# Linear attention: the key-value product folded into the output weight, denominators by column-tiled matmuls, their inverses broadcast by DMA onto the query features

## Chip, cores, metric

One core of one Trainium2 chip. The metric is device time in microseconds (us). "Clock" is the granted TensorE clock that the trace records, 1.00 being full speed. PE is the matrix engine, DVE the vector engine, ACT the scalar engine, POOL GpSimd, SP the engine that issues DMA here, PEld the weight loads of PE. PE writes its results to PSUM, which is used here in banks of 128x512 values. A q behind an engine's name (SPq) marks its sequencer, which waits and issues DMA.

## The reference

Two pre-layernorm blocks follow each other: a linear attention (S = 2048 tokens, D = 1024, 32 heads of 32) and a token-mixing MLP (F = 3584), called the mixer below. Only the end of the attention matters here:

```python
phi = lambda t: jnp.where(t > 0, t + 1, jnp.exp(t)) + 1e-6
pq, pk = phi(q), phi(k)
kv  = jnp.einsum("bhsd,bhse->bhde", pk, v)          # per head 32x32
z   = jnp.einsum("bhsd->bhd", pk)
num = jnp.einsum("bhqd,bhde->bhqe", pq, kv)
den = jnp.einsum("bhqd,bhd->bhq", pq, z)[..., None] + 1e-6
o   = num / den
h   = x + o.transpose(...).reshape(B, S, D) @ wo
# then h2 = h + MLP over tokens of layernorm(h)
```

## The kernel before

Queries are made in 32 units (u, j): 512 tokens (block u of 4) by 128 features (j of 8). Each unit is eight 128x512 matmuls into a PSUM bank, then phi: two ACT operations, then two DVE operations that write `pqT`.

```python
def phi_parts(dst, src, n, pool):
    ...
    def act():
        pin(nc.scalar.activation(e_sb[:], src, ACT.Exp))
        pin(nc.scalar.activation(r_sb[:], src, ACT.Relu))
    def dve():
        pin(nc.vector.tensor_scalar(e_sb[:], e_sb[:], 1.0, PHI_EPS, ALU.min, ALU.add))
        pin(nc.vector.tensor_tensor(dst, e_sb[:], r_sb[:], ALU.add))
def q_unit(u, j):
    qp = acc_tile()                       # one of five PSUM banks
    for kt in range(ND):
        nc.tensor.matmul(qp[:, 0:SW], lhsT=wq_sb[:, kt, j*P:(j+1)*P],
                         rhs=xnT[:, kt, u*SW:(u+1)*SW], start=(kt == 0), stop=(kt == ND-1))
    phi_evac(pqT[:, j, u*SW:(u+1)*SW], qp[:, 0:SW], SW, a2k)   # a2k: four buffers
```

`pin` keeps an operation where the program has it. The others may be reordered on their engine by the compile-time scheduler. Then, for each of 16 tiles of 128 tokens, small matmuls give numerator and denominator side by side; the division and a DMA transpose put o where `pqT` was; the output projection follows.

```python
def attn_num_den(i):
    for j in range(ND):
        nc.tensor.matmul(nd_ps[:, b, sl*NCOL:(sl+1)*NCOL],           # 128 x 132
                         lhsT=pqT[:, j, i*P:(i+1)*P], rhs=ndrhs[:, j, :], start=True, stop=True)
    # ACT: rd = exp(-ln(den)); DVE: o_sb = num * rd (three operations out of PSUM)
    ...
def attn_transpose(i, o_sb):
    nc.sync.dma_start_transpose(out=pqT[:, :, i*P:(i+1)*P], in_=o_sb[:])
...
for (u, j) in q_units[8:]:
    q_unit(u, j)
    if u >= 1 and j % 2 == 1:
        attn((u - 1) * TPC + j // 2)      # attn = attn_transpose(i, attn_num_den(i))
        ...                               # weight loads
for i in range(NS):
    if i % 2 == 0 and i // 2 < TPC:
        attn(NS - TPC + i // 2)
    ...
    out_proj(i)                           # two groups of eight 128x512 matmuls with wo_sb
    ...
```

## Time and profile before

| | before |
|---|---|
| time, median (range) | 573.22 us (573.16 to 573.3, 3 runs) |
| span profiled | 571.5 us |
| PE / DVE / ACT busy | 99% / 68% / 48% |
| from the first query unit after the last kv accumulation to the first matmul of the mixer | 125.92 to 235.50 us |

The last row is the stage that the change touches; I call it "the stage". In it all numbers are taken from PE's timeline, from the start of one group of matmuls to the start of the next.

A stretch of nearly the whole stage, kernel before. The columns are the stretch and its length, busy time and (instructions) of PE, PEld, DVE, ACT and POOL, then granted clock, DMA share, GB/s.

```profile
126.00:236.00 110.00, 110.00 (x605) 53.59 (x603) 86.35 (x210) 74.80 (x179) 0.00 (x0) 1.00 0.61 157
```

PE's timeline before around one group of the small matmuls: start, duration (both us), engine, line, operation, output and inputs, shapes, count.

```profile
136.75 1.89 PE L1019 MATMUL acc_t<-xnT,wq_sb 128*128 128x512 bf16 x8
138.47 0.63 PE L1118 MATMUL nd_ps<-ndrhs,pqT 128*128 128x132 bf16 x8
138.94 1.24 PE L1019 MATMUL acc_t<-xnT,wq_sb 128*128 128x512 bf16 x5
```

PE never pauses in the stage, at full clock. A group of eight small matmuls lasts 0.63 us, but what follows it starts 138.94 - 138.47 = 0.47 us after it: durations overlap, so costs on PE must be read from starts. Sixteen such groups are 16 x 0.47 = 7.5 us.

### The profile page before, as it was taken

Reading aid. Unit: us, or ns where it says so; the run is one execution under the profiler, and the core shown is the slowest. Engines: PE = TensorE matmul, PEld = TensorE weight load, DVE = VectorE, ACT = ScalarE, POOL = GpSimd, SP = SyncE. Lnnn points to the kernel's source line nnn. Section 1 sums busy time; section 2 is a strip of 40 time slices with the busy share of each in tenths; the row PEclk is TensorE's granted clock in tenths of the full one; section 3 lists DMA queues with packets and bytes.
Section 4 is the critical chain, followed back from the end, with each engine's and each line's share of the span. In section 5 each row is a group of like instructions: output and inputs, shape, how many; then the busy total and the mean of one; then the engine's idle time right before and its main releaser. Section 6 shows DMA issues by size and latency. Waiting matters only on the chain.

```text
span 571.5 us, 8308 instructions
## 1 busy us (share of the span) xinstructions
PE 563.7 (99%) x3124; PEld 293.3 (51%) x3124; DVE 390.2 (68%) x759; ACT 272.0 (48%) x585; POOL 1.8 (0%) x8
## 2 busy tenths in 40 slices
PE   7999999999999999999999999999999999999997
PEld 3444444455554444346555565555445655645643
DVE  6898887546767879873735627453979749659625
ACT  4747777666667776445445354453220411311211
POOL 1000000000000000000000000000000000000000
PEclk9999999999999999999999999999999999999999
DMA  9933432029536753104041340413892932912111
GB/s 303 357 76 79 89 74 38 19 96 323 118 72 127 177 178 111 55 2 147 1 148 28 120 148 1 148 48 81 205 255 84 244 96 75 278 56 73 38 47 46
DMA packets 97800, 66.61 MB, mean 117 GB/s; under 512 B 32082, under 2 KB 91744, under 8 KB 97760
## 3 DMA queue, kind: packets, MB, share of 16 engines
q1 hardware_dynamic: 97024, 65.42, 41.7%
q10 hardware_dynamic: 672, 0.66, 0.3%
q8 instruction: 24, 0.39, 0.3%
q14 instruction: 16, 0.13, 0.1%
q0 software_dynamic: 64, 0.01, 0.0%
HBM read 50.34 MB, written 8.39 MB: 103 GB/s over the span
## 4 chain that ended last, share of the span: by engine, by line
PE 95%; DVE 3%; ACT 1%; issue 1%; DMA 1%; ACTq 0%
PE psB L297 10%; PE psC L297 10%; PE acc_t L1019 9%; PE acc_t L1167 9%; PE psC L208 7%; PE psA L297 7%; PE psI L230 7%; PE psB L208 6%; PE psI L208 6%; PE psB L750 4%; PE psC L750 4%; PE psA L750 4%; PE psA L208 3%; PE acc_t L674 2%; PE psE L750 2%; PE psE L297 1%
## 5 line engine op out<-in xcount | busy, mean ns | idle before, releaser
L297 PEld LDWEIGHTS <-sa 128*128 128x128 f16 x436 | 42.6, 98 | 46.8 <-issue 0.7
L1019 PE MATMUL acc_t<-xnT,wq_sb 128*128 128x512 bf16 x256 | 58.0, 379 | 0.0
L1167 PE MATMUL acc_t<-wo_sb,pqT 128*128 128x512 bf16 x256 | 56.1, 379 | 0.0
L208 PEld LDWEIGHTS <-wq 128*128 128x128 bf16 (+1 forms) x357 | 34.5, 98 | 31.3
L297 PEld LDWEIGHTS <-wq 128*128 128x128 bf16 (+1 forms) x324 | 31.6, 98 | 33.1 <-issue 1.0
L208 PE MATMUL psC<-gs,wq 128*128 128x512 f16 (+2 forms) x210 | 45.0, 365 | 0.0
L1167 PEld LDWEIGHTS <-pqT 128*128 128x128 bf16 x256 | 24.8, 98 | 29.0
L1019 PEld LDWEIGHTS <-wq_sb 128*128 128x128 bf16 x256 | 24.5, 98 | 27.4
L166 ACT ACTIVATE e_sb<-acc_t 128x512 bf16<-128x512 f32 x40 | 23.9, 597 | 26.5 <-PE acc_t L1019 24.3
L170 DVE TENSOR_SCALAR e_sb<-e_sb 128x512 bf16<-128x512 bf16 x64 | 18.5, 289 | 25.4 <-ACT e_sb L166 24.8
L208 PEld LDWEIGHTS <-sa 128*128 128x128 f16 x231 | 22.6, 98 | 18.6
L750 PEld LDWEIGHTS <-xs 128*128 128x128 f16 x208 | 20.0, 98 | 23.3 <-DVE xs L736 1.3
L208 DVE TENSOR_TENSOR ot<-ot,hr 128x512 bf16<-128x512 bf16 (+2 forms) x27 | 11.2, 415 | 28.1 <-ACT ot L406 27.7
L333 ACT COPY psC<-psB 128x512 f32<-128x512 f32 x22 | 12.5, 570 | 35.1 <-PE psB L297 21.5
L297 PE MATMUL psB<-hT,sa 128*128 128x512 f16 x112 | 28.4, 379 | 0.0
L441 DVE TENSOR_TENSOR e<-psI,es 128x256 f32<-128x256 f32 x12 | 5.1, 425 | 34.0 <-PE psI L230 34.0
L297 PE MATMUL psC<-hT,wq 128*128 128x512 f16 x112 | 28.3, 379 | 0.0
L750 PE MATMUL psA<-wkv,xnT 128*128 128x512 bf16 x104 | 26.7, 379 | 0.0
L1178 DVE BATCH_NORM_STATS2 hst<-acc_t 128x6 f32<-128x512 f32 x32 | 22.1, 692 | 6.7 <-ACT h_bf L1177 6.5
L297 PE MATMUL psA<-hO,wq 128*128 128x512 f16 x112 | 25.6, 379 | 0.7 <-ACT psB L316 0.7
L297 PE MATMUL psB<-hO,sa 128*128 128x512 f16 x112 | 25.5, 379 | 0.0
L297 PE MATMUL psC<-hT,sa 128*128 128x512 f16 x112 | 25.5, 379 | 0.0
(184 smaller groups left out, 1022.9 us busy)
## 6 DMA issues: line engine op xcount, KB each, us to landing
wq<-in_B_w_dram SPq DMA_DIRECT2D x14, 1024.0 KB, 7.7
wq<-in_B_w_dram SPq DMA_DIRECT2D x8, 1792.0 KB, 9.1
xr<-in_A_x_dram SPq DMA_DIRECT2D x16, 256.0 KB, 3.1
h_dram<-h_bf SPq DMA_DIRECT2D x16, 256.0 KB, 2.2
hr<-h_dram SPq DMA_DIRECT2D x32, 128.0 KB, 2.4
out_dram<-ot SPq DMA_DIRECT2D x31, 128.0 KB, 1.8
x_sb<-in_A_x_dram SPq DMA_DIRECT2D x15, 256.0 KB, 3.2
wkv<-in_A_wqkv_dram SPq DMA_DIRECT2D x2, 1024.0 KB, 9.0
```

What stands on the lines that cost most here:

```text
L166: pin(nc.scalar.activation(e_sb[:], src, ACT.Exp))
L170: pin(nc.vector.tensor_scalar(e_sb[:], e_sb[:], 1.0, PHI_EPS, ALU.min, ALU.add))
L208: return (lambda *a, **kw: pin(op(*a, **kw))) if Held.on else op
L230: pe.matmul(ps, lhsT=self.lhs[m][:, k, :], rhs=self.mov[m][:, k, :], start=(start and k == 0), stop=(k == self.nk - 1), skip_group_check=True,
L297: pe.matmul(ps[:, cols], lhsT=lhs[:, k, :], rhs=mv(k)[:, cols], start=(start and k == 0), stop=(k == self.nk - 1), skip_group_check=True,)
L333: nc.scalar.copy(self.C[:], self.B[:])
L441: dve.tensor_tensor(self.sts[m].e[:, self.cols(h)], ps, es, ALU.add)
L674: mm = nc.tensor.matmul(pp[:, 0:CW], lhsT=xnT[:, kt, i * P:(i + 1) * P], rhs=wkv[:, kt, c * CW:(c + 1) * CW], start=(kt == 0), stop=(kt == ...
L750: pin(nc.tensor.matmul(ps[:], lhsT=lhs[:, k, :], rhs=rhs[:, k, :], start=(start and k == 0), stop=(k == hk2 - 1), skip_group_check=True,))
L1019: nc.tensor.matmul(qp[:, 0:SW], lhsT=wq_sb[:, kt, j * P:(j + 1) * P], rhs=xnT[:, kt, u * SW:(u + 1) * SW], start=(kt == 0), stop=(kt == ND ...
L1167: nc.tensor.matmul(ap_[:, 0:CW], lhsT=pqT[:, j, i * P:(i + 1) * P], rhs=wo_sb[:, j, dc * CW:(dc + 1) * CW], start=(j == 0 and not SEED_RES ...
L1178: nc.vector.bn_stats(st[:, dc, :], ap_[:, 0:CW])
```

## The change

The intent: (phi(q) kv / den) @ wo equals (phi(q) / den) @ (kv @ wo). So kv, a block-diagonal matrix, is multiplied into wo once (16 matmuls, "the fold"), and the numerator matmuls go. Denominators are made for a whole block of 512 tokens: eight 128x512 matmuls with 32 output columns each, four of them side by side in the array. Their inverses lie in 8 of the 32 rows of each column tile, one row a head; each row has to reach the 32 partitions of its head. They are stored to DRAM and read back broadcast, and one DVE multiplication a block scales `pqT`. The diff, cut to its core:

```diff
-            def attn_num_den(i):
-                for j in range(ND):
-                    nc.tensor.matmul(nd_ps[...], lhsT=pqT[:, j, ...], rhs=ndrhs[:, j, :], start=True, stop=True)
-                ...                                   # Ln, Exp, three DVE multiplications, DMA transpose
+            def fold(j):
+                for c in range(NDC):
+                    ps = acc_tile()
+                    nc.tensor.matmul(ps[:, 0:CW], lhsT=kvT[:, j, :], rhs=wo_sb[:, j, cols], start=True, stop=True)
+                    ...                               # copied over wo_sb as fp16 by ACT (c = 0) and DVE (c = 1)
+            def den(u):
+                ps = ndp.tile([P, SW], F32, tag="den", name="den_ps")
+                for o in range(2):
+                    for g in range(4):
+                        j = 2 * g + o
+                        nc.tensor.matmul(ps[g * QR:(g + 1) * QR, :],
+                            lhsT=zz[:, j, (1 - o) * HB:(1 - o) * HB + QR], rhs=pqT[:, j, u * SW:(u + 1) * SW],
+                            start=(o == 0), stop=(o == 1), skip_group_check=True, tile_position=(0, g * QR))
+                rd = a3d.tile([P, SW], FP16, tag="rd", name="rd")
+                nc.scalar.activation(ps[:], ps[:], ACT.Ln, bias=eps_den[:], scale=1.0 / S)
+                nc.scalar.activation(rd[:], ps[:], ACT.Exp, scale=-1.0)
+                nc.sync.dma_start(rd_dram[u][:], rd[:])
+                rdb = a3d.tile([P, ND, SW], FP16, tag="rdb", name="rdb")       # one buffer
+                for j in range(ND):
+                    r0 = (j // 2) * QR + (j % 2) * HB
+                    nc.sync.dma_start(rdb[:, j, :],
+                        rd_dram[u][r0:r0 + HB, :].unsqueeze(1).to_broadcast([HB, DH, SW]))
+                rdbs[u] = rdb
+            def scale_q(u):
+                v = pqT[:, :, u * SW:(u + 1) * SW]
+                nc.vector.tensor_tensor(v, v, rdbs.pop(u)[:], ALU.mult)
...
+            den(0)
             for n, (u, j) in enumerate(q_units[8:]):
                 q_unit(u, j)
-                if u >= 1 and j % 2 == 1:
-                    attn(...); ...
+                if n == 0: kv_transpose()
+                elif n % 2 == 1 and n < 8: load_w1(*divmod(n // 2, 2))
+                if 4 <= n < 4 + ND: fold(n - 4)
+                if j == 5: scale_q(u - 1)
+                if j == ND - 1: den(u)
...
             for i in range(NS):
-                if i % 2 == 0 and i // 2 < TPC: attn(NS - TPC + i // 2)
+                if i == 4: scale_q(NSC - 1)
```

More of the change, by code (lines that the diff above doesn't have):

```diff
@@ L56 @@
     HB = P // DH
-    NCOL = P + HB
-    JPB = BANK // NCOL
-    NNB = (ND + JPB - 1) // JPB
+    QR = P // 4
+    assert ND == 8 and 3 * HB <= QR
     KPB = BANK // (P + 1)
@@ L100 @@
     for q in range(HB):
-        nc.vector.memset(maskbd[q * DH:(q + 1) * DH, q * DH:(q + 1) * DH], 1.0)
+        nc.vector.memset(maskbd[q * DH:(q + 1) * DH, q * DH:(q + 1) * DH], 1.0 / S)
         nc.vector.memset(m4[q * DH:(q + 1) * DH, q:q + 1], 1.0)
@@ L107 @@
     eps_den = const.tile([P, 1], F32)
-    nc.vector.memset(eps_den[:], DEN_EPS)
+    nc.vector.memset(eps_den[:], DEN_EPS / S)
     b1_rows = const.tile([NF, P], BF16)
@@ L585 @@
         a3s = actx.enter_context(tc.tile_pool(name="a3s", bufs=4))
-        a3w = actx.enter_context(tc.tile_pool(name="a3w", bufs=3))
-        a3o = actx.enter_context(tc.tile_pool(name="a3o", bufs=3))
+        a3d = actx.enter_context(tc.tile_pool(name="a3d", bufs=1))
         hstat = actx.enter_context(tc.tile_pool(name="hstat", bufs=1))
@@ L594 @@
         pqT = pqpool.tile([P, ND, S], BF16)
-        ndrhs = pqpool.tile([P, ND, NCOL], BF16)
+        kvbd = pqpool.tile([P, ND, P], BF16)
+        kvT = pqpool.tile([P, ND, P], FP16)
+        zz = pqpool.tile([P, ND, QR + HB], BF16)
         xctx = ExitStack()
@@ L1084 @@
                 q_fill()
+            nc.vector.memset(zz[:, :, 0:3 * HB], 0.0)
+            nc.vector.memset(zz[:, :, 3 * HB:], float(S))
             for b in range(NKB):
@@ L1087 @@
                 nc.vector.tensor_tensor(
-                    ndrhs[:, j0:j0 + n, 0:P],
+                    kvbd[:, j0:j0 + n, :],
                     kv_ps[b][:, 0:n, 0:P],
@@ L1093 @@
                 nc.vector.tensor_tensor(
-                    ndrhs[:, j0:j0 + n, P:NCOL],
+                    zz[:, j0:j0 + n, HB:2 * HB],
                     kv_ps[b][:, 0:n, P:P + 1].to_broadcast([P, n, HB]),
@@ L1109, with kv_transpose @@
         ndp = a3p.enter_context(tc.tile_pool(name="ndp", bufs=1, space=PSUM))
-        nd_ps = ndp.tile([P, NNB, BANK], F32, name="nd_ps")
-        nc.vector.memset(nd_ps[:], 0.0)
+        rd_dram = [dram.tile([P, SW], FP16, name=f"rd_dram{u}") for u in range(NSC)]
         with ExitStack() as a3:
-            def attn_num_den(i):
+            def kv_transpose():
+                tp = ndp.tile([P, ND, P], BF16, tag="tp", name="kvtp")
                 for j in range(ND):
-                    b, sl = divmod(j, JPB)
-                    nc.tensor.matmul(
-                        nd_ps[:, b, sl * NCOL:(sl + 1) * NCOL],
-                        lhsT=pqT[:, j, i * P:(i + 1) * P],
-                        rhs=ndrhs[:, j, :],
-                        start=True,
-                        stop=True,
-                    )
-                dn = a3s.tile([P, NNB * JPB * HB], F32, name="dn")
-                nc.scalar.activation(
-                    dn[:].rearrange("p (b s c) -> p b s c", b=NNB, c=HB),
-                    nd_ps[:, :, 0:JPB * NCOL].rearrange("p b (s c) -> p b s c", c=NCOL)[:, :, :, P:NCOL],
-                    ACT.Ln,
-                    bias=eps_den[:],
-                    scale=1.0,
-                )
-                rd = a3s.tile([P, NNB * JPB * HB], F32, name="rd")
-                nc.scalar.activation(rd[:], dn[:], ACT.Exp, scale=-1.0)
-                o_sb = a3o.tile([P, D], BF16, name="o_sb")
-                for b in range(NNB):
-                    nsl = min(JPB, ND - b * JPB)
-                    blk = nd_ps[:, b, 0:nsl * NCOL].rearrange("p (s c) -> p s c", c=NCOL)
-                    nc.vector.tensor_tensor(
-                        o_sb[:, b * JPB * P:(b * JPB + nsl) * P].rearrange("p (s h e) -> p s h e", h=HB, e=DH),
-                        blk[:, :, 0:P].rearrange("p s (h e) -> p s h e", e=DH),
-                        rd[:, b * JPB * HB:(b * JPB + nsl) * HB].rearrange("p (s h) -> p s h", h=HB).unsqueeze(3).to_broadcast([P, nsl, HB, DH]),
-                        ALU.mult,
-                    )
-                return o_sb
-            def attn_transpose(i, o_sb):
-                nc.sync.dma_start_transpose(out=pqT[:, :, i * P:(i + 1) * P], in_=o_sb[:])
@@ new lines, in kv_transpose @@
+                    nc.tensor.transpose(tp[:, j, :], kvbd[:, j, :], ident[:])
+                nc.scalar.copy(kvT[:], tp[:])
+            wf = wo_sb[:].bitcast(FP16)
+            def fold(j):
+                for c in range(NDC):
+                    cols = slice(c * CW, (c + 1) * CW)
+                    ps = acc_tile()
+                    nc.tensor.matmul(ps[:, 0:CW], lhsT=kvT[:, j, :], rhs=wo_sb[:, j, cols], start=True, stop=True)
+                    if c == 0:
+                        nc.scalar.copy(wf[:, j, cols], ps[:, 0:CW])
+                    else:
+                        nc.vector.tensor_copy(wf[:, j, cols], ps[:, 0:CW])
@@ new lines @@
+            rdbs = {}
+            def den(u):
[3 more added lines that the diff above has]
+                        j = 2 * g + o
+                        nc.tensor.matmul(
+                            ps[g * QR:(g + 1) * QR, :],
+                            lhsT=zz[:, j, (1 - o) * HB:(1 - o) * HB + QR],
+                            rhs=pqT[:, j, u * SW:(u + 1) * SW],
+                            start=(o == 0),
+                            stop=(o == 1),
+                            skip_group_check=True,
+                            tile_position=(0, g * QR),
+                        )
+                rd = a3d.tile([P, SW], FP16, tag="rd", name="rd")
[5 more added lines that the diff above has]
+                    r0 = (j // 2) * QR + (j % 2) * HB
+                    nc.sync.dma_start(
+                        rdb[:, j, :],
+                        rd_dram[u][r0:r0 + HB, :].unsqueeze(1).to_broadcast([HB, DH, SW]),
+                    )
+                rdbs[u] = rdb
@@ L1169, in out_proj @@
                             lhsT=pqT[:, j, i * P:(i + 1) * P],
-                            rhs=wo_sb[:, j, dc * CW:(dc + 1) * CW],
+                            rhs=wf[:, j, dc * CW:(dc + 1) * CW],
                             start=(j == 0 and not SEED_RESIDUAL),
@@ L1192, in normalize_h @@
                     combine(hE[:, q, :], hO[:, q, :], hT2[:, q, :], hT3[:, q, :], hT4[:, q, :])
-            def attn(i):
-                attn_transpose(i, attn_num_den(i))
             TPC = SW // P
+            for c in range(NDC):
+                load_wo(c)
             for i in range(XRL):
                 load_xr(i)
-            for (u, j) in q_units[8:]:
+            den(0)
+            for n, (u, j) in enumerate(q_units[8:]):
                 q_unit(u, j)
-                if u >= 1 and j % 2 == 1:
-                    i = (u - 1) * TPC + j // 2
-                    attn(i)
-                    if i % 2 == 1 and i // 2 < 2:
-                        load_wo(i // 2)
-                    elif i % 2 == 1 and i // 2 < 6:
-                        load_w1(*divmod(i // 2 - 2, 2))
+                if n == 0:
+                    kv_transpose()
+                elif n % 2 == 1 and n < 8:
+                    load_w1(*divmod(n // 2, 2))
+                if 4 <= n < 4 + ND:
+                    fold(n - 4)
+                if j == 5:
+                    scale_q(u - 1)
+                if j == ND - 1:
+                    den(u)
             xctx.close()
+            a3w = a3.enter_context(tc.tile_pool(name="a3w", bufs=3))
             hpool = mctx.enter_context(tc.tile_pool(name="hpool", bufs=1, side="right"))
@@ L1217 @@
             for i in range(NS):
-                if i % 2 == 0 and i // 2 < TPC:
-                    attn(NS - TPC + i // 2)
+                if i == 4:
+                    scale_q(NSC - 1)
                 if i + XRL < NS:
```

## The prediction

> What bounds the kernel now. The page shows PE busy 563.7 of 571.5 us (99%) at full granted clock; DVE 68%, ACT 48%. The chain of waits is 95% PE. The change touches only the stage from the last kv accumulation (126 us) to the end of the output projection (236 us). In the windows 126-178 and 178-236 PE is always busy, and PE's waits name nothing there above 0.5 us. So a change is worth what it does to PE's issue time, unless it makes a new wait.
>
> What goes. 128 matmuls 128x132. The profile gives 221 ns each, but that is latency: in the chain a group of eight pushes the next matmul back by 0.47 us, 59 ns each. So 16 x 0.47 = 7.5 us of PE, plus one 0.47 us PE wait on DVE at 181.3. Off the path go 48 DVE multiplies out of PSUM (about 21 us), 32 short ACT operations (9 us), a 1.34 us memset and 16 DMA transposes.
>
> What comes, on PE:
> - 16 folding matmuls 128x512. 256 such take 55.3 us in the chain (216 ns each): 3.45 us.
> - 8 transposes, about 59 ns each by the above: 0.5 us.
> - Denominators: 32 matmuls 128x512, in 8 groups of four column tiles. Serial: 6.9 us. The Trainium skill (TensorEngine Tiling (Array Packing), Overview) gives up to 4x, and its Key Properties says a change of tiling mode drains the array. No run here shows either yet. Estimate: 0.23-0.28 us a group, plus about 0.16 us of drain (379 less 216 ns) on each side of four blocks: 3.1-3.5 us.
> PE sum: -8.0 + 3.45 + 0.5 + 3.3 = -0.7 us.
>
> Off the path: DVE gets 4 scalings of 128x4096 (estimate from 0.42 us for 512 and 0.69 for 1024 elements: 2.3 us each, 9 us) and 8 evictions (5 us): about 9 us less than before. ACT stays about level.
>
> The new risk is latency. Denominators -> Ln, Exp (1.2 us) -> DMA out (2.2 us, as h_dram) -> 8 broadcast reads -> scaling on the in-order DVE. The reads have four head rows outermost; by the Trainium skill (DMA: Bandwidth & Descriptors, "How many engines (k)") such a transfer uses 4 of 16 engines. Estimate: 366 GB/s at about 126-135 us is 23 GB/s an engine; 1 MB on four takes 11-12 us. About 16 us from denominators to scaling. In the first three blocks the scaling stands six query units later (10.4 us): DVE stalls some 5 us, but four phi buffers and five PSUM banks let PE run on 7 us or more. For the last block it stands at output tile 4, about 14 us after the queries end. DVE may stall 3-6 us and then scale for 2.3 us while PE has five banks of 1.73 us to fill. I allow 0-2 us there, partly as a later hand-over to the mixer (PE waits 0.9 us there now).
>
> Prediction: 572.6 us (573.2 - 0.7 + about 0.1 for waits), 80% range 570.4 to 575.8. Faster by over 2%: 0.01; within: 0.97; slower: 0.02.
>
> What would show it: PE busy down 0-2 us; the four denominator blocks delaying the next matmul by 0.6-1.0 us each; folds at 216 ns; DVE busy down about 9 us; broadcasts landing in 5-12 us; scaling about 2.3 us; PE waits on DVE around output tiles 4-8 below 2 us.
>
> What would make it wrong: column tiles not running together (+4 us); the denominators stuck behind the last phi (2 us each time); broadcasts slower than estimated, so that DVE stops freeing PSUM banks (several us); scaling at half the rate (2 us more each); or a schedule that moves the output projection or weight loads.

## More of the kernel before

Lines of the page of the kernel before: span and instructions, busy time, granted clock in tenths over 40 slices (9 is 90% or more), instruction fetches among the DMA queues (queue, packets, MB, share), and the chain of waits by engine.

```profile
span 571.5 us, 8308 instructions
PE 563.7 (99%) x3124; PEld 293.3 (51%) x3124; DVE 390.2 (68%) x759; ACT 272.0 (48%) x585; POOL 1.8 (0%) x8
PEclk9999999999999999999999999999999999999999
q8 instruction: 24, 0.39, 0.3%
PE 95%; DVE 3%; ACT 1%; issue 1%; DMA 1%; ACTq 0%
```

## The result, and the profile after

After: 614.74 us, median of 4 runs (614.16 to 616.64), against 573.25 us for before in the same rounds. The ratio is 1.073, 95% interval 1.0706 to 1.0753. Slower by 7.3%; predicted was no difference, with 2% given to "slower". Ratios here are the mean time of one kernel's fast runs over that of the other's of the same rounds, so they are not quite the ratio of the medians quoted.

The same lines of the page as before, kernel after:

```profile
span 612.7 us, 8144 instructions
PE 575.6 (94%) x3052; PEld 290.2 (47%) x3052; DVE 381.9 (62%) x724; ACT 274.5 (45%) x570; POOL 1.8 (0%) x8
PEclk9999999999688697999999999999999999999999
PE 68%; DVE 12%; DMA 10%; ACT 3%; SPq 3%; issue 3%; DVEq 0%; ACTq 0%
```

DVE's busy time fell by 8.3 us, as predicted (9), and that bought nothing. The chain now passes through DVE and DMA for a fifth of the span, and the clock has dips. PE's waits after (engine, what waits, for what: us in total, times, longest us), and the first below is all that DVE waits for the broadcasts in the stage:

```profile
DVE pqT L1165 <- DMA rdb<-rd_dram: 33.3, 4, 9.5
...
PE den_ps L1141 <- DVE pqT L170: 22.7, 5, 9.6
PE acc_t L1184 <- ACT acc_t L1182: 5.5, 1, 5.5
```

PE waits 22.7 us in front of denominator matmuls, for phi's last DVE operation (line 170), and 5.5 us in the output projection. The timeline after shows why. In brackets stands how long the engine was idle just before, and what ended it.

```profile
132.75 0.39 PE L1141 MATMUL den_ps<-pqT,zz 128*32 128x512 bf16 x1
...
133.17 0.66 ACT L1151 ACTIVATE den_ps<-den_ps,eps_den 128x512 f32<-128x512 f32 x1 [0.96 <-PE den_ps L1141]
...
134.49 0.34 SPq L1153 DMA_DIRECT2D rd_dram<-rd  x1
...
138.78 6.64 SPq L1157 DMA_DIRECT2D rdb<-rd_dram  x8
...
148.08 0.40 PE L1141 MATMUL den_ps<-pqT,zz 128*32 128x512 bf16 x3
...
154.27 2.29 DVE L1165 TENSOR_TENSOR pqT<-pqT,rdb 128x4096 bf16<-128x4096 bf16 x1 [9.51 <-DMA rdb<-rd_dram]
156.48 0.42 DVE L170 TENSOR_TENSOR pqT<-e_sb,r_sb 128x512 bf16<-128x512 bf16 x1
...
158.08 0.62 PE L1141 MATMUL den_ps<-pqT,zz 128*32 128x512 bf16 x4 [9.61 <-DVE pqT L170]
158.64 2.31 PE L1019 MATMUL acc_t<-xnT,wq_sb 128*128 128x512 bf16 x5
```

Read it downwards. Denominators of block 0 are complete by 133.1; Ln and Exp follow; the store is issued at 134.49, the broadcasts from 138.78 on. DVE reaches the scaling (line 1165) and stands there for 9.51 us, until the last broadcast has landed and it starts at 154.27: 15.5 us after the first was issued. Only after the scaling does DVE do the phi additions queued behind it (156.48 and on). PE has meanwhile begun the denominators of block 1 (148.08): the compile-time scheduler put the first three of them before the last query unit's phi was there. The fourth needs a phi addition that stands behind the scaling. PE is in order, so it stops: 9.61 us. Then the denominators of block 1 finish, and their store and broadcasts start only now. It is a closed loop. The stores show its period: 134.49, 162.84, 187.84, 214.20 us, so 28.4, 25.0 and 26.4 us apart, where a block of eight query units costs PE 13.8 us.

The chain of waits after says the same in its own words, in order of time (start, us, what):

```profile
144.18 9.87 DMA rdb<-rd_dram
...
154.27 0.06 DVE pqT L1165
...
156.48 0.42 DVE pqT L170
...
157.62 0.43 DVE pqT L170
...
158.08 0.62 PE den_ps L1141 x4
```

Three stretches after, columns as for the stretch before:

```profile
126.00:274.00 148.00, 119.82 (x527) 50.13 (x526) 77.29 (x170) 77.85 (x163) 0.00 (x0) 0.88 0.37 120
158.60:161.00 2.40, 2.40 (x10) 0.69 (x6) 0.66 (x3) 0.00 (x0) 0.00 (x0) 0.50 0.00 0
164.60:178.50 13.90, 12.53 (x59) 5.45 (x58) 4.24 (x10) 9.03 (x17) 0.00 (x0) 1.00 0.24 77
```

The second stretch follows a PE wait of 9.6 us: the clock granted is 0.50, and five query matmuls take 2.31 us where before they took 1.24. The trace's clock records have four such stretches in the stage, of 10.24, 6.83, 10.24 and 6.83 us. Each begins during a PE wait (of 9.6, 4.5, 6.8 and 5.5 us), 2.1 to 4.3 us after PE stopped, and goes on for 3.4 us or more after PE has started again. The Trainium skill (TensorE: Matmul & The Clock Gate, "Part 1: The HAM clock gate") says that the array runs at half rate after a window of about 3.4 us without activity, and needs about as long of activity to come back. This trace agrees in part: the half clock comes with the waits and lasts two or three times 3.41 us. But 3.4 us without activity are not needed: in e1, e2 and e3 below, waits of 2.3 to 2.4 us are each followed by 3.41 us at 0.50, while the waits of 1.2 to 1.3 us in e2, e5 and e8 are not. So a wait on PE costs more than its length. The third stretch is one in which only broadcasts run: 0.24 of the sixteen DMA engines' time, 77 GB/s, close to four of sixteen engines. The Trainium skill (DMA: Bandwidth & Descriptors, "How many engines (k)", in the section on the semaphore increment of 16) says that a transfer uses as many engines, up to 16, as divide the slowest dimension of both sides: here 4, the heads. The trace agrees with 4, and its semaphore records show it directly: when a broadcast lands, four updates come (for the last one of block 0 at 153.76 to 154.05 us); in e2 below, with another shape, sixteen come. Nor does the issuing set the pace: of block 1's eight broadcasts seven are issued by 168.54 us, when one has landed, and the others then land 1.43 us apart.

Where the 41.2 us of span (612.7 - 571.5) are, from PE's timeline:

| | before | after | difference |
|---|---|---|---|
| the stage | 109.58 (125.92 to 235.50) | 148.58 (125.74 to 274.32) | +39.0 |
| of it: PE waits | 0 | 22.67 + 5.5 | +28.2 |
| of it: low clock (query matmuls 47.24 to 50.17, projection 55.37 to 59.57, denominators 3.66 to 6.50, fold 3.55 to 3.71) | | | +10.1 |
| of it: arithmetic (-7.52 small matmuls, +3.66 denominators, +3.55 fold, +0.45 transposes, +0.65 query matmuls, -0.10 projection) | | | +0.7 |
| the stage's start, and the mixer up to its first `psI` matmul | | | +0.1 |
| the mixer from its first `psI` matmul to the end | 312.2 | 314.3 | +2.1 |

The stage's -0.18 us of start is in the last but one row. The times at full clock, from which the low-clock row starts, are those of e6 below, where PE never waits and the clock is 1.0. There the query matmuls take 0.65 us more than before (47.24 against 46.59), mostly because each that precedes a piece of the denominators holds PE for 309 ns in place of 216. A second estimate of the low clock, from the clock records: 19.3 us of the four stretches lie outside the waits, and at half the clock half of that is lost, 9.7 us.

### The profile page after: what moved, and what is told of

The parts are those of the page before. It is cut to its first block, busy times and chain, and to the rows that moved or that the text cites. A ratio compares the mean times of both kernels' runs of the same rounds, so it can differ in the third digit from the quotient of the medians.

```text
span 612.7 us, 8144 instructions
## 1 busy us (share of the span) xinstructions
PE 575.6 (94%) x3052; PEld 290.2 (47%) x3052; DVE 381.9 (62%) x724; ACT 274.5 (45%) x570; POOL 1.8 (0%) x8
## 4 chain that ended last, share of the span: by engine, by line
PE 68%; DVE 12%; DMA 10%; ACT 3%; SPq 3%; issue 3%; DVEq 0%; ACTq 0%
PE psB L296 7%; PE psC L296 7%; PE psC L207 7%; PE psB L207 6%; DMA rdb<-rd_dram 6%; PE psI L207 5%; PE psA L296 5%; PE psI L229 5%; PE psB L750 4%; PE psC L750 4%; PE acc_t L1019 4%; PE psA L750 4%; SPq L1157 3%; DMA wq<-in_B_w_dram 3%; PE psA L207 3%
## 5 line engine op out<-in xcount | busy, mean ns | idle before, releaser
L1184 PE MATMUL acc_t<-wo_sb,pqT 128*128 128x512 f16 x256 | 59.8, 398 | 5.5 <-ACT acc_t L1182 5.5
L1019 PE MATMUL acc_t<-xnT,wq_sb 128*128 128x512 bf16 x256 | 61.6, 393 | 0.0
L1165 DVE TENSOR_TENSOR pqT<-pqT,rdb 128x4096 bf16<-128x4096 bf16 x4 | 9.2, 2292 | 33.3 <-DMA rdb<-rd_dram 33.3
L332 ACT COPY psC<-psB 128x512 f32<-128x512 f32 x22 | 12.5, 570 | 36.4 <-PE psB L296 22.9
L296 PE MATMUL psB<-hT,sa 128*128 128x512 f16 x112 | 28.4, 379 | 0.0
L1141 PE MATMUL den_ps<-pqT,zz 128*32 128x512 bf16 x32 | 7.0, 501 | 22.7 <-DVE pqT L170 22.7
L1182 ACT CAST acc_t<-xr 128x512 f32<-128x512 bf16 x32 | 18.8, 589 | 19.8 <-DVE hst L1195 19.6
```

What stands on the lines that cost most here:

```text
L296: pe.matmul(ps[:, cols], lhsT=lhs[:, k, :], rhs=mv(k)[:, cols], start=(start and k == 0), stop=(k == self.nk - 1), skip_group_check=True,)
L332: nc.scalar.copy(self.C[:], self.B[:])
L1019: nc.tensor.matmul(qp[:, 0:SW], lhsT=wq_sb[:, kt, j * P:(j + 1) * P], rhs=xnT[:, kt, u * SW:(u + 1) * SW], start=(kt == 0), stop=(kt == ND ...
L1182: nc.scalar.copy(ap_[:, 0:CW], xr[:, dc * CW:(dc + 1) * CW])
L1184: nc.tensor.matmul(ap_[:, 0:CW], lhsT=pqT[:, j, i * P:(i + 1) * P], rhs=wf[:, j, dc * CW:(dc + 1) * CW], start=(j == 0 and not SEED_RESIDUAL),
```

## The experiments

The theory, called A in the expectations: a loop of latency. The broadcasts, slow because they use four DMA engines, hold the in-order DVE at the scaling; the phi additions stand behind it; the next denominators need them; PE stops, and the low clock follows from that. The rivals: that the column-tiled denominators or their mode changes cost PE this much, or lower the clock themselves; that it is the traffic of the broadcasts rather than the waiting for them; or that only the place of the scaling in DVE's order matters and the broadcasts' speed does not.

In what follows the diffs are against the kernel after, if nothing else is said. "Stage" is the time of the stage from PE's timeline. Before's medians of the same rounds were 573.15 us (e1 to e4), 573.33 (e5 to e8), 573.26 (e9 to e11) and 573.25 (e12).

| run | what | us, median (range) | ratio to before, 95% | stage, us | PE waits in it, us |
|---|---|---|---|---|---|
| after | | 614.74 (614.16 to 616.64) | 1.073 (1.0706 to 1.0753) | 148.58 | 28.2 |
| e1 | scaling doesn't read the broadcasts (wrong result) | 584.8 (584.32 to 586.35) | 1.0208 (1.0193 to 1.0223) | 114.43 | 2.3 |
| e2 | broadcasts shaped for 16 engines | 583.23 (582.25 to 584.01) | 1.0171 (1.0154 to 1.0188) | 118.53 | 5.8 |
| e3 | scaling after the next denominators | 588.8 (588.1 to 589.96) | 1.0275 (1.026 to 1.029) | 123.68 | 8.9 |
| e4 | scaling on POOL | 602.92 (600.82 to 604.71) | 1.0518 (1.0485 to 1.0552) | 136.62 | 18.8 |
| e5 | e2 and e3 together | 576.6 (575.98 to 576.73) | 1.0051 (1.0038 to 1.0064) | 111.59 | 1.2 |
| e6 | no store, no broadcasts (wrong result) | 576.36 (576.05 to 576.8) | 1.005 (1.0036 to 1.0064) | 110.26 | 0 |
| e7 | every broadcast twice | 644.13 (643.4 to 646.98) | 1.1243 (1.1213 to 1.1272) | 178.81 | 59.4 |
| e8 | e5, denominators one unit later | 575.37 (575.03 to 575.49) | 1.003 (1.0018 to 1.0043) | 110.13 | 1.2 |
| e9 | e8 with 80 more PE instructions at the start | 573.31 (573.27 to 573.36) | 0.9999 (0.9987 to 1.0011) | 110.13 | 1.2 |
| e10 | e9 with a source line moved that had no effect | 573.27 (573.19 to 573.41) | 0.9999 (0.9987 to 1.0011) | 110.13 | 1.2 |
| e11 | before, 34 more PE instructions | 573.07 (573.01 to 575.12) | 1.0004 (0.9992 to 1.0015) | 109.56 | 0 |
| e12 | before, 112 more PE instructions | 575.12 (574.61 to 576.04) | 1.0036 (1.0023 to 1.005) | 109.58 | 0 |

All results but those of e1 and e6 are correct.

### e1: the scaling reads ones, the broadcasts run unread

```diff
+            ones = a3d.tile([P, SW], FP16, name="ones")
+            nc.vector.memset(ones[:], 1.0)
...
-                nc.vector.tensor_tensor(v, v, rdbs.pop(u)[:], ALU.mult)
+                rdbs.pop(u)
+                nc.vector.tensor_tensor(v, v, ones[:].unsqueeze(1).to_broadcast([P, ND, SW]), ALU.mult)
```

> Wrong on purpose: the scaling multiplies by a constant tile of ones; denominators, their DMA to DRAM and the broadcasts still run, nothing waits for the broadcast. Theory A (the in-order DVE, waiting for the broadcast, holds back the last phi that the next denominators on PE need; the clock drop follows from PE's idling): about 572 to 574 us, PE idle within 1 us of before, granted clock 0.99 or more, PE waits on pqT gone. Rival B (folding, column tiling or their mode changes are what costs, and lower the clock): still above 600 us with clock near 0.97. Rival C (the broadcasts or the earlier weight loads hurt as DMA traffic): still above 590 us.

Measured: 584.8 us. All denominators, folds, scalings and DMA are as after, and 30 of the 41 us are gone, with every PE wait on phi. The granted clock is 1.00 from 126 to 178 us, so column tiling does not lower it. That the time does not come to before's had a cause I had not expected, which ACT's and PE's waits show:

```profile
ACT h_bf L1197 <- DMA h_dram<-h_bf: 6.4, 1, 6.4
...
PE psE L296 <- DVE hE L155: 3.1, 1, 3.1
PE acc_t L1187 <- ACT acc_t L1185: 2.3, 1, 2.3
```

ACT waits 6.4 us for the store of an output tile (`h_bf`) to leave its buffer. That store was issued on the same queue behind the last block's broadcasts, and landed 8.7 us after its issue, where before the median is 2.2. Twelve of its sixteen semaphore updates came within 3.4 us of the issue, the last four only after 8.4 to 8.7: as many as there are engines in a broadcast. PE loses 2.3 us there (the last line), about as much again at the low clock (1.8 us in the projection, against e6), and 3.1 us at the mixer's beginning, where 1.5 were lost after. So the broadcasts hurt in a second way, as traffic, but a small one.

### e2: broadcasts with the heads inside and 32 partitions outside

```diff
-                for j in range(ND):
-                    r0 = (j // 2) * QR + (j % 2) * HB
-                    nc.sync.dma_start(rdb[:, j, :],
-                        rd_dram[u][r0:r0 + HB, :].unsqueeze(1).to_broadcast([HB, DH, SW]))
+                by_head = rd_dram[u][:].rearrange("(g r) s -> r g s", g=4)
+                rdb_v = rdb[:].rearrange("p (g o) s -> p o g s", o=2)
+                for o in range(2):
+                    for q in range(HB):
+                        nc.sync.dma_start(rdb_v[q * DH:(q + 1) * DH, o, :, :],
+                            by_head[o * HB + q:o * HB + q + 1, :, :].to_broadcast([DH, 4, SW]))
...
-                nc.vector.tensor_tensor(v, v, rdbs.pop(u)[:], ALU.mult)
+                mul = nc.vector.tensor_tensor(v, v, rdbs.pop(u)[:], ALU.mult)
+                if u < NSC - 1:
+                    pin(mul)
```

The same bytes in the same number of transfers, but each has 32 partitions as its slowest dimension. The scaling is pinned, so that it stays before the next denominators as after.

> Same bytes, same 1 KB rows, still eight broadcasts a block, but each writes 32 partitions of one head for four feature blocks, so that both sides' outermost dimension is 32 and not 4; the scaling keeps its place before the last phi. If the 4-engine shape is what makes the broadcast long: the first-issue-to-scaling time falls from about 15 us to 6-8 us, DMA share during the broadcasts rises from about 0.26 to over 0.5, PE waits on pqT fall from 22.7 us to under 4, time 573 to 580. If the latency is in the issue of eight DMAs or in DRAM round trips: above 600.

Measured: 583.23 us, 3 above the range expected. From the first broadcast of the second block to its scaling are 7.7 us (160.58 to 168.28), against 13.9 after, with a DMA share of 0.53 against 0.24. PE's waits, and one line of ACT's timeline:

```profile
PE acc_t L1188 <- ACT acc_t L1186: 2.5, 2, 1.3
PE acc_t L1019 <- ACT r_sb L166: 2.4, 1, 2.4
...
PE den_ps L1141 <- DVE pqT L170: 0.2, 1, 0.2
```

```profile
175.44 0.66 ACT L1151 ACTIVATE den_ps<-den_ps,eps_den 128x512 f32<-128x512 f32 x1 [8.52 <-PE den_ps L1141]
```

The wait that cost 22.7 us is down to 0.2. What is left comes from the same loop one engine on: ACT, in order too, sat 8.52 us at the Ln of the next denominators, ahead of exponentials that PE's banks needed. Bandwidth is a lever; the order is still wrong.

### e3: each scaling behind the next block's denominators

```diff
+            rdb2 = xctx.enter_context(tc.tile_pool(name="rdb2", bufs=1))
...
-                rdb = a3d.tile([P, ND, SW], FP16, tag="rdb", name="rdb")
+                rdb = (rdb2 if u % 2 == 0 else a3d).tile([P, ND, SW], FP16, tag="rdb", name="rdb")
...                                           # the scaling pinned, as in e2
                 q_unit(u, j)
+                if j == ND - 1:
+                    den(u)
+                    scale_q(u - 1)
...
-                if j == 5:
-                    scale_q(u - 1)
-                if j == ND - 1:
-                    den(u)
```

The slow broadcast stays; a second buffer lets two blocks be under way. (Unpinned, the scheduler may place the scaling elsewhere, as e10 shows; no run has this kernel without the pin.)

> Broadcast shape as in the change (4 engines); only the scaling of block u-1 is held on DVE until after the last phi of block u (and a second buffer, so that the next broadcast need not wait for it). Theory A: the PE waits of the denominators on phi (22.7 us) fall under 3 us although each broadcast still takes about 15 us; what stays is the wait at output tile 4 for the last block (5.5 us or less); time 575 to 584. If instead the slow broadcast costs by any other way than that order: above 600.

Measured: 588.8 us. PE's waits:

```profile
PE acc_t L1187 <- ACT acc_t L1185: 6.5, 1, 6.5
PE acc_t L1128 <- DVE wo_sb L1132: 2.4, 1, 2.4
```

The wait of the denominators for phi is gone altogether, although the first block's broadcasts still take 15.9 us from the first issue to the scaling: the order, with the second buffer, breaks the loop, so the slow broadcast is not enough by itself to make it. It still shows where nothing can hide it: at the last block, in the output projection (6.5 us), and once when DVE stood at a scaling and a fold's PSUM bank was not copied out (2.4 us). I had put this kernel some 5 us lower: I had not counted these two.

### e4: the scaling on POOL

```diff
...                                           # second buffer as in e3
-                nc.vector.tensor_tensor(v, v, rdbs.pop(u)[:], ALU.mult)
+                nc.gpsimd.tensor_tensor(v, v, rdbs.pop(u)[:], ALU.mult)
```

This takes the scaling out of DVE's order by giving it to an idle engine.

> The scaling moved from DVE to the idle Pool engine (with the second buffer), broadcast unchanged. Theory A: DVE never waits for the broadcast, PE waits on phi gone, time 573 to 585, depending on how long Pool takes for 128x4096 (unknown here; over about 10 us the last block would hold up output tile 12). Otherwise above 600.

Measured: 602.92 us. A miss, for a reason outside both theories. The timeline of POOL and DVE:

```profile
154.71 7.92 POOL L1166 TENSOR_TENSOR pqT<-pqT,rdb 128x4096 bf16<-128x4096 bf16 x1 [151.87 <-DMA rdb<-rd_dram]
154.80 8.11 DVE L170 TENSOR_TENSOR pqT<-e_sb,r_sb 128x512 bf16<-128x512 bf16 x1
...
172.13 7.75 DVE L169 TENSOR_SCALAR e_sb<-e_sb 128x512 bf16<-128x512 bf16 x1 [0.81 <-ACT e_sb L165]
```

While POOL ran its 7.92 us, a DVE addition that takes 0.42 us elsewhere took 8.11, and a `TENSOR_SCALAR` of 0.29 us took 7.75: DVE stood still until POOL was through, and PE behind it. The Trainium skill (SBUF — State Buffer, "SBUF: two separate sides") says so: the port pair that the two engines share is an exclusive lock, and whoever comes second is fully blocked; it counts for DVE operations in a two-port performance mode, and for those with two SBUF inputs when the POOL operation reads SBUF. The trace agrees. The experiment says nothing for or against theory A; DVE was held as before, only by something else.

### e5: e2 and e3 together

No new edit: e2's broadcasts, e3's order, pin and second buffer.

> Both repairs together: the 32-partition broadcast of e2 and the scaling behind the last phi with a second buffer of e3. Theory: no PE wait over 1.5 us in the attention stage, clock 0.995 or more, 574 to 578 us: the change's arithmetic is level with before, so not faster than before's 573.2.

Measured: 576.6 us, clock 0.999. The only PE wait left in the stage is 1.17 us, in the output projection:

```profile
PE acc_t L1189 <- ACT acc_t L1187: 1.2, 1, 1.2
```

Both parts are needed: each alone leaves 583 and 589. Of the 41 us of excess, 38 went with them.

### e6: neither store nor broadcasts

```diff
...                                           # the ones of e1
-                nc.sync.dma_start(rd_dram[u][:], rd[:])
-                rdb = a3d.tile([P, ND, SW], FP16, tag="rdb", name="rdb")
-                for j in range(ND):
-                    ...
-                rdbs[u] = rdb
```

> Wrong on purpose, as e1, but now neither the denominators' store nor the broadcasts are issued at all. e1 kept 2.3 us of PE wait that its trace puts on h_bf's store, landing late behind the broadcast on the same DMA queue. If that reading is right: this wait goes, the attention stage (first extra query unit to first mixer matmul) is within 1.5 us of before's 109.6 us (arithmetic so far: -7.5 for the old matmuls, +3.7 denominators, +3.6 fold, +0.45 transposes = +0.2 us), total 573 to 577 with about 2 us of it after the attention. If folding or tiling have a cost of their own: above 580.

Measured: 576.36 us. Its output is wrong, which doesn't matter for the time. Clock 1.0, no PE wait in the stage, which lasts 110.26 us, 0.7 longer than before. The 6.4 us wait of ACT for the store of `h_bf`, seen in e1, is gone. So the whole of the change's arithmetic on PE costs 0.7 us, and the rival of the tiling cost falls. e5, which gives the correct result, takes as long in all as this kernel without transfers, and 1.3 us longer in the stage, of which 1.2 us is the wait shown above: little of the broadcast is left to gain. But both are 3 us over before, and the stage accounts for only 0.7 to 2.0 of that. The rest is in the mixer, whose code the change does not touch.

### e7: each broadcast issued twice

```diff
-                for j in range(ND):
+                for j in [*range(ND), *range(ND)]:
```

> Everything as in the change, but each broadcast is issued twice into the same tile. If the loop broadcast -> scaling -> last phi -> denominators -> next broadcast sets the pace, each of the four rounds grows by about one more broadcast time (7 to 15 us): 645 to 680 us. If the broadcasts' length is not what PE waits for: within 10 us of 614.7.

Measured: 644.13 us, 29 us more than after and just below the range expected. PE's waits:

```profile
PE den_ps L1141 <- DVE pqT L170: 46.1, 3, 17.2
PE acc_t L1184 <- ACT acc_t L1182: 13.2, 1, 13.2
```

The same two waits, doubled and more: 46.1 and 13.2 us against 22.7 and 5.5. The stores' period goes to 37.1, 33.2 and 36.4 us, so 8 to 10 us a block more for another copy of its broadcasts. The loop's length is set by the broadcasts.

### e8: e5 with each block's denominators one query unit later

Against e5:

```diff
                 if j == ND - 1:
-                    den(u)
                     scale_q(u - 1)
+                if j == 0 and u >= 2:
+                    den(u - 1)
...
             for i in range(NS):
-                if i == 4:
+                if i == 1:
+                    den(NSC - 1)
+                if i == 6:
                     scale_q(NSC - 1)
```

After the change the scheduler cut denominators into pieces (7 and 1, or 3, 4 and 1), each with a change of tiling mode on either side. One unit later all of phi is there.

> e5, and the denominators of block u one query unit later, so that their eight matmuls run in one piece (e1: a block cut into 7 + 1 costs 0.87 us) and never wait for the last phi; last scaling at output tile 6 in place of 4. Expected 0.5 to 1.5 us under e5: 573 to 577 us. Best hope for a version level with before; none below 571.

Measured: 575.37 us. The stage is 110.13 us, 0.55 longer than before, with the 1.17 us wait still in it. From the second block on, PE's timeline has the denominators in one piece of eight, after which the next matmul starts 0.55 us later (the first two lines below, e8). Cut in two (the others, after, block 0) they cost 0.546 + 0.323 = 0.87 us. In both kernels the matmul before each piece holds PE 0.09 us longer, which makes 0.64 and 1.06 us.

```profile
149.96 0.61 PE L1142 MATMUL den_ps<-pqT,zz 128*32 128x512 bf16 x8
150.51 0.61 PE L1128 MATMUL acc_t<-wo_sb,kvT 128*128 128x512 bf16 x2
...
131.02 0.61 PE L1141 MATMUL den_ps<-pqT,zz 128*32 128x512 bf16 x7
131.56 1.25 PE L1019 MATMUL acc_t<-xnT,wq_sb 128*128 128x512 bf16 x5
...
132.75 0.39 PE L1141 MATMUL den_ps<-pqT,zz 128*32 128x512 bf16 x1
133.07 0.82 PE L1019 MATMUL acc_t<-xnT,wq_sb 128*128 128x512 bf16 x3
```

Eight serial 128x512 matmuls would be 8 x 0.216 = 1.73 us, so four column tiles gave 1.73 / 0.64 = 2.7 times, mode changes included. The Trainium skill (TensorEngine Tiling (Array Packing), "Theoretical Speedup" and "Key Properties") gives up to 4 times, and says that a change of mode drains the array. The trace agrees with the first, 2.7 times being under 4. It fits the second: the matmul before each piece holds PE for 309 ns in place of 216. The mixer, from its first `psI` matmul to the end, is 314.0 us against 312.2: that is all that now separates e8 from before.

### e9: e8 with the PE program shifted by 80 instructions

What could lengthen untouched code? In both traces the mixer waits for its weights, 2 MB a load: DVE waits for weight DMA 9.5 us in all before and 13.1 after, and the added time comes in two steps of about 1 us. The records of DMA transfers show, among the load's packets, instruction fetches of 16 KB (the row of queue q8 on the page of before: 24 packets, 0.39 MB). The Trainium skill (Runtime: NRT & Kernel Launch, "Instruction fetch mechanics") has instruction memory refilled in blocks of 16 KiB, or 256 instructions, and calls the cost "mostly hidden". With 72 matmuls and 72 weight loads fewer than before, PE reaches the ends of these blocks at other moments. So e9 only makes the warm-up at the start of the program longer in instructions and equal in time, against e8:

```diff
-            warm_up(10)
+            warm_up(50, 104)
```

> Question: the 2 us that every variant loses inside the mixer, 40 us and more after the attention. Traces so far: a 2 MB weight load takes 6.6 to 6.9 us, but 7.6 to 8.3 us whenever a 16 KB instruction fetch falls inside it; in before none does, in the variants two do. e9 is e8 with the 10 warm-up matmuls of 512 columns replaced by 50 of 104 columns (same time, 80 more PE instructions), so the fetches come about 7 us earlier and miss the loads. If the fetches are the cause: the mixer from its first inner product to the end takes 312.2 to 312.8 us as in before (e8: 314.0), total 573.0 to 574.0. If not: as e8, 575.4.

Measured: 573.31 us against 573.26 for before, and 2.1 less than e8 in an earlier set of rounds. The mixer takes 312.3 us again. The fetches next to the five 2 MB weight loads, from the DMA records (each pair: duration of the load in us, and when after its start a fetch began, "none" if there was none within the load or 3 us of it):

```text
before: 6.64 none | 6.77  9.43 | 6.68  7.55 | 6.82  6.33 | 6.56  6.40
after : 6.76 6.59 | 8.10  5.30 | 8.04  5.24 | 7.09 -0.31 | 6.86 -1.36
e8    : 6.74 6.46 | 7.91  4.84 | 8.04  0.12 | 7.07 -0.36 | 6.86 -1.11
e9    : 6.62 -1.7 | 6.93  none | 6.66  none | 6.94  none | 6.80  none
e12   : 6.57 6.21 | 7.67  4.97 | 7.92  4.84 | 7.02 -0.49 | 6.69 -1.56
```

A load with a fetch inside takes 7.7 to 8.1 us, one without 6.6 to 6.9, and one with a fetch begun half a microsecond before it 7.0 to 7.1. Two long loads, two steps of 1 us. A fetch that falls in a load's last half microsecond does nothing. (The 256 instructions of a fetch come out of the trace too: 24 fetches of 16 KB for before's 3124 matmuls and 3124 weight loads are 260 each.)

### e10: e9 with the last scaling moved in the source

```diff
-                if i == 6:
+                if i == 8:
                     scale_q(NSC - 1)
```

This was to remove the 1.17 us wait left in the output projection.

> e9 with the last block's scaling at output tile 8 in place of 6 (out of the way of the broadcast; e8 still waited 1.2 us there). Expected 0.5 to 1.2 us under e9: 572.0 to 573.5, that is, level with before or up to 0.2% faster. Above 574 would say the 1.2 us had another cause.

Measured: 573.27 us. The gain expected did not come, because the edit had no effect: this scaling is not pinned, and the compile-time scheduler put it at the same place (198.52 us in e9, 198.42 in e10, where all of PE's stage starts 0.1 us earlier). So e10 is a repeat of e9. That wait seems to come from the 2.29 us that the scaling itself keeps DVE from freeing a bank, which was not tested.

### e11 and e12: the kernel before with its PE program shifted

If fetches inside loads cost 2 us, then before can be made slower in the same way. Both edits are against before; the warm-up's columns are cut so that its time stays about equal.

```diff
-            warm_up(10)
+            warm_up(27, 192)          # e11
```

> The kernel before with 27 warm-up matmuls of 192 columns in place of 10 of 512 (34 more PE instructions, same time, nothing else). Its instruction fetches, 6.3 to 7.6 us after the start of the weight loads now, come about 3 us earlier, into the loads. If that is what costs: 1 to 3 us slower than before, 574.3 to 576. If not: 573.2 within 0.3.

Measured: 573.07 us. Inconclusive: the fetches moved by less than I had reckoned, to 6.4 to 6.7 us after the start of four of the loads, which is their last moment (they take 6.7 to 6.8 us), and nothing changed.

```diff
-            warm_up(10)
+            warm_up(66, 78)           # e12
```

> e11 missed: its traces show the fetches only about 1 us earlier, at 6.4 to 6.7 us after the load's start, at its very end. The change has 144 PE instructions fewer than before, which is 112 more modulo the 256 that a 16 KB fetch of 64-byte instructions holds (an estimate). This run is the kernel before with 66 warm-up matmuls of 78 columns in place of 10 of 512: 112 more PE instructions, same time. If the phase of the fetches costs the 2 us, two loads should now take 7.6 to 8.3 us and the total be 574.7 to 575.7; if the fetches fall inside and the time stays at 573.2 within 0.3, the theory is wrong; if they again fall outside, it says nothing.

Measured: 575.12 us, ratio 1.0036 (1.0023 to 1.005). The fetches fell at 4.97 and 4.84 us into the second and third load, which took 7.67 and 7.92 us (last row of the table above). The kernel before, with the same work in all but the warm-up, is 2 us slower, as after and e8 are in their mixers. (The execution profiled was the fastest, 574.61 us; its mixer takes 313.5 us, 1.3 more than before's.) What the fetch does to the load (for instance which transfers it displaces) no run shows.

## Why the prediction was wrong

Right were the sizes of the single parts. Folding matmuls took 216 to 222 ns (predicted 216). A denominator block cut in two put off the next matmul by 0.87 us, 1.06 with the longer matmuls before its pieces (0.6 to 1.0). The scalings took 2.29 us each (2.3). DVE's busy time fell by 8.3 us (9). Right too was where the danger lay, that the transfers use four engines, and their rate: 1.43 us each in block 1, 11.4 us for eight (11 to 12).

**The step that failed** is this one: "DVE stalls some 5 us, but four phi buffers and five PSUM banks let PE run on 7 us or more." It counts what the query matmuls need, free banks. But PE is in order, and among the query matmuls stand the denominators, which need the phi additions themselves; those stand behind the stalled scaling. PE's slack was not 7 us of buffers but the distance to the next denominators: in block 1 DVE went idle at 144.76 us and PE stopped at 148.48, 3.7 us later. The trace has PE stopped there five times, 22.7 us in all, and e2 (shorter broadcast), e3 (other order) and e7 (longer broadcast) moved exactly this wait: 0.2, 0 and 46.1 us. The prediction even listed "the denominators stuck behind the last phi (2 us each time)" among its dangers, without seeing that the phi in question would itself be stuck behind the scaling, which makes it a loop: each block's broadcasts start only when the previous block's have been used.

Terms that were mis-sized or absent:

- The way from the denominators to the scaling: 16 us predicted, 21.2 us measured in block 0 (133.07 to 154.27). From the store's issue to the first broadcast's were 4.3 us (2.2 predicted), and 15.5 us from there to the scaling (11 to 12): 3.9 us pass before the first broadcast lands. DVE's stall was up to 9.5 us, not 5.
- PE's arithmetic: -0.7 us predicted, +0.7 measured (e6). The denominators, cut into two pieces or more in every block, took 4.3 us with the longer query matmuls around them, not 3.3. And 0.47 us of the saving was no wait of PE's: the trace has it at the weight loads, and PE has none in the stage before.
- The last block: 0 to 2 us predicted, 5.5 us measured.
- The clock: not in the prediction at all. The waits brought it to 0.50 four times, at about 10 us.
- The mixer: "a schedule that moves the output projection or weight loads" was among the dangers, but what moved was the fetching of instructions: +2.1 us (e9, e12).

Shown: the loop, its two levers (e2, e3, e5, e7), that the arithmetic is nearly level (+0.7 us, e6), the 2 us of the fetches (e9, e12). Worked out and not tested separately: the 10 us of low clock, as the growth of the same matmuls' time; e1 to e3, e5 and e8 agree in that it shrinks with the waits.

No version beat before. The best correct ones, e9 and e10, are equal to it (0.9999). PE bounds this stage, the change exchanges 7.5 us of small matmuls for 7.7 us of others (6.4 with most denominators in one piece, as in e8) and for 0.4 to 0.65 us of longer query matmuls beside them, and the DVE time that it frees was free already. Even without the 1.17 us wait that is left it would be an estimated 0.2%.

## What to carry to other kernels

When new work makes a round trip through other engines and DRAM, don't ask only how many buffers lie between it and the bounding engine; follow the in-order queues and ask whether something behind the wait feeds the next start of the same round trip. If so, its latency is paid once per turn, and the cure is order (use the result one turn later, with a second buffer) together with a transfer shape that uses all DMA engines; here 41 us shrank to 3 by those two. And count what the bounding engine loses on top of a wait: the clock fell to half in four waits of 4.5 to 9.6 us, which made 28 us of waits cost 38.

## What the Trainium skill lacked or had wrong

- "Runtime: NRT & Kernel Launch", "Instruction fetch mechanics", calls the cost of an instruction block boundary mostly hidden. Here a 16 KB fetch inside a 2 MB weight load went with 7.7 to 8.1 us of load instead of 6.6 to 6.9, and two of them made the kernel 2 us slower (e8 against e9: 575.37 and 573.31 us; e12 against before: 575.12 and 573.25 us). The page says nothing of what a fetch does to transfers under way. That a change in one stage's number of PE instructions can move the time of another stage is on no page I read.
- "DMA: Bandwidth & Descriptors" gives the number of engines a transfer uses, but no figure for what a four-engine transfer costs later ones on the same queue: the store of an output tile landed 8.7 us after issue behind the broadcasts (e1), with a median of 2.2 us before.
- "TensorE: Matmul & The Clock Gate" and "TensorEngine Tiling (Array Packing)" have no measured figure for four column tiles at 512 columns (the first has one for three), nor for a change of mode: here 0.64 us for eight matmuls in one piece, 2.7 times as fast as serially, and 1.06 us when cut in two; 0.09 us of each piece is the longer matmul before it.
- "TensorE: Matmul & The Clock Gate" does not give the shortest wait that can bring the clock down: here waits of 2.3 to 2.4 us were followed by 3.41 us at half clock (e1, e2, e3).
